# Hidden DFT of three chunks as seven half-size block products, on one Trainium2 core

## The chip, the core and the metric

The kernel runs on one core of a Trainium2 chip. The time is that of the device in microseconds, from a median of repeated executions. Five engines work beside each other, each through its own instructions in order: TensorE (PE, with its weight loads PEld), VectorE (DVE), ScalarE (ACT), GpSimd (POOL) and SyncE (SP), which here only issues DMAs. An instruction that waits for a semaphore holds back everything behind it on its engine.

## What is computed

Four layers, alternating: a Fourier mixing layer A and an MLP layer B, each behind a layer norm, with the residual added. Only A is touched:

```python
def _A_ref(x, dft_seq_re, dft_seq_im, dft_hid_re, dft_hid_im):
    a = jnp.einsum("bsd,ed->bse", x, dft_hid_re)
    b = jnp.einsum("bsd,ed->bse", x, dft_hid_im)
    y = jnp.einsum("ts,bse->bte", dft_seq_re, a) - jnp.einsum("ts,bse->bte", dft_seq_im, b)
    return y
...
x = x + _A_ref(_layernorm(x, axis=-1), A_dft_seq_re, A_dft_seq_im, A_dft_hid_re, A_dft_hid_im)
```

x is 2048 x 512 in float32. The kernel applies the sequence DFT first and the hidden DFT (512 x 512, real and imaginary) after it.

## The kernel before

**Precision.** Every float32 factor is split in two: a "high" part, a cast to fp32r on ACT, and a "low" part, what the cast lost, a subtraction on DVE. A product is three matmuls: high x high, high x low, low x high (`mm3`, L316 to L318).

**Chunks.** The 2048 rows go as four chunks of 512 (c = 0 to 3). The sequence DFT of chunk c takes an x phase (`x_phase`, L498) and a y phase (`y_phase`, L531). The results stand in SBUF as four sums: `im0`, `re1`, `im1`, `re0`. The hidden DFT of chunk c-1 runs inside the x phase of chunk c, as eight calls of `hid` (L593) of 12 matmuls 128x512 each, placed by `HAT` (L40): four calls sum into the two banks PD for the first half of the rows, four for the second.

**The stream.** DFT matrices come as pieces of 512 KB into four raw places (`raw`), DMAs issued by SP. Each becomes one or two *items*, split into a ring of four slots (`ring`). An x phase has 16 items: an even one (kind "plain") feeds 12 matmuls, an odd one (kind "one", a difference of the two halves) 6; in between stand the `hid` calls, each with an item of its own. A y phase has 16 items (`by1`, `by0`) of 12 matmuls. With each item that PE takes (`stream`, L304), the code issues the first stage of the item three further on (`stage_one`: on ACT the cast L260, or on DVE the difference L262 or L266 and then the cast L263 or L267) and the second stage of the item before that one (`stage_two`: DVE low part, L279). A slot is written again when PE is done with the item four back, so both engines wait for PE in the stream. A raw place is loaded again when the stages that read it have been issued.

**Other work beside the stream.** `late` holds lists of functions; `run_late(n)` (L493) issues list n behind item n of the x phase. They hold the last additions to the four sums (L491), their highs (L449) and lows (L452). `add_y` adds the hidden DFT's banks to the residual rows (in `tmp`, called X1) and `y_stats` takes layer norm statistics of them.

What the order of the code is on each engine is the order in which they run: there is no scheduler (`manual_schedule`).

## Time and profile before

| what | value |
|---|---|
| median of 3 runs (lowest to highest) | 1429.8 us (1428.65 to 1429.96) |
| profiled execution: its time, its span | 1430.81 us, 1428.8 us |
| granted TensorE clock over the span | 1.000 |
| DMA moved | 302.13 MB, mean 211 GB/s |
| x phase of chunk 2 in layer 0 | 193.0 to 247.4 us |
| x phases of chunks 1 and 2 in layer 1 | 802.4 to 856.8 us, 900.4 to 954.8 us |

The profiled execution took 1430.81 us, of which 1428.8 us lie between its first and its last instruction; the remaining 2.0 us lie around them. It stands 1.0 us over the median. The busy time of PE says that a matmul was in flight, not that it ran at full rate: matmuls overlap, so their rate is read from one start to the next. Phases are told apart by the tiles of the matmuls: `ax` in an x phase, `ay` in a y phase, `rr` as the stationary operand in the hidden DFT.

### The profile page before, as it was taken

The numbers are of one execution on the slowest core, as the hardware profiler recorded it, in microseconds if no ns is written. First come the engines' busy times: TensorE is split into PE (matmuls) and PEld (weight loads), VectorE is DVE, ScalarE is ACT, GpSimd is POOL, SyncE is SP. The second block draws the span as 40 slices with busy tenths as digits, with TensorE's granted clock in tenths as the row PEclk, the third lists the DMA queues.
The fourth block names the chain that finished last, engine by engine and source line by source line (L and its number), as shares of the span: only waits on it lengthen the run. The fifth ranks groups of instructions, "written<-read, shape, count | busy, mean of one in ns | idle before, by whom it ended". The sixth has DMA issues, their size and how long they took to land.

```text
span 1428.8 us, 17276 instructions
## 1 busy us (share of the span) xinstructions
PE 1422.0 (100%) x6258; PEld 1174.2 (82%) x6258; DVE 1147.5 (80%) x1603; ACT 726.3 (51%) x977; POOL 79.9 (6%) x111
## 2 busy tenths in 40 slices
PE   9999999999999999999999999999999999999998
PEld 7888888888888888888888888888888888888887
DVE  7876997988869888677889979888889698637586
ACT  5553454455465745345554544544555576333352
POOL 2100000001002000000000000000000010000000
PEclk9999999999999999999999999999999999999999
DMA  7426646657664859968755566565676468666594
GB/s 243 140 89 207 206 166 203 204 167 245 225 205 111 287 201 321 379 215 319 240 174 195 168 191 204 186 199 190 205 258 225 137 164 303 209 196 260 168 312 144
DMA packets 136813, 302.13 MB, mean 211 GB/s; under 512 B 15372, under 2 KB 61196, under 8 KB 133528
## 3 DMA queue, kind: packets, MB, share of 16 engines
q1 hardware_dynamic: 132504, 298.93, 63.1%
q10 hardware_dynamic: 4224, 2.10, 0.5%
q8 instruction: 49, 0.80, 0.2%
q14 instruction: 36, 0.29, 0.1%
HBM read 246.18 MB, written 54.81 MB: 211 GB/s over the span
## 4 chain that ended last, share of the span: by engine, by line
PE 95%; DVE 3%; DMA 2%; issue 0%; SPq 0%; ACT 0%; DVEq 0%
PE psd L318 10%; PE psd L316 10%; PE psd L317 10%; PE psa L316 9%; PE psa L318 9%; PE psa L317 9%; PE psc L317 6%; PE psc L318 6%; PE psc L316 6%; PE psb L317 6%; PE psb L318 6%; PE psb L316 6%; DMA raw<-in_ws 1%; DVE ring L279 1%; DMA xs<-in_x 1%; DVE ring1f L266 0%
## 5 line engine op out<-in xcount | busy, mean ns | idle before, releaser
L260 ACT CAST ring<-raw 128x1024 fp32r<-128x1024 f32 x127 | 133.0, 1052 | 98.9 <-PE psd L318 50.1
L279 DVE TENSOR_TENSOR ring<-raw,ring 128x1024 fp32r<-128x1024 f32 (+1 forms) x128 | 154.5, 1211 | 22.5 <-ACT ring L260 22.4
L316 PE MATMUL psd<-ring,rr 128*128 128x512 f32 x208 | 80.9, 389 | 0.0
L317 PE MATMUL psd<-ring,rr 128*128 128x512 f32 x208 | 80.9, 389 | 0.0
L318 PE MATMUL psd<-ring,rr 128*128 128x512 f32 x208 | 80.9, 389 | 0.0
L360 POOL TENSOR_TENSOR rs<-ve,mhalf 128x4 f32<-128x4 f32 x16 | 28.7, 1794 | 578.2 <-DVE nm L359 578.2
L267 ACT CAST ring<-ring0f 128x1024 fp32r<-128x1024 f32 x28 | 29.5, 1054 | 57.1 <-DVE ring0f L266 57.1
L279 DVE TENSOR_TENSOR ring<-ring1f,ring 128x512 fp32r<-128x512 f32 (+1 forms) x56 | 53.2, 949 | 0.8 <-ACT ring L263 0.8
L339 POOL TENSOR_TENSOR rs<-ve,mhalf 128x2 f32<-128x2 f32 (+1 forms) x33 | 30.1, 911 | 396.3 <-DVE nb L338 396.3
L317 PE MATMUL psc<-ring,ay 128*128 128x512 f32 x128 | 50.0, 391 | 0.9 <-DVE ring L279 0.9
L317 PE MATMUL psb<-ring,ay 128*128 128x512 f32 x128 | 50.1, 392 | 0.0
L318 PE MATMUL psc<-ring,ay 128*128 128x512 f32 x128 | 49.8, 389 | 0.0
L318 PE MATMUL psb<-ring,ay 128*128 128x512 f32 x128 | 49.8, 389 | 0.0
L316 PE MATMUL psb<-ring,ay 128*128 128x512 f32 x128 | 49.8, 389 | 0.0
L316 PE MATMUL psc<-ring,ay 128*128 128x512 f32 x128 | 49.8, 389 | 0.0
L267 ACT CAST ring<-ring1f 128x1024 fp32r<-128x1024 f32 x28 | 29.5, 1055 | 39.6 <-DVE ring1f L266 39.6
L317 PE MATMUL psa<-ring,ay 128*128 128x512 f32 x126 | 49.0, 389 | 0.0
L316 PE MATMUL psa<-ring,ay 128*128 128x512 f32 x126 | 49.0, 389 | 0.0
L318 PE MATMUL psa<-ring,ay 128*128 128x512 f32 x126 | 49.0, 389 | 0.0
L316 PE MATMUL psd<-ring,ay 128*128 128x512 f32 x126 | 49.0, 389 | 0.0
L317 PE MATMUL psd<-ring,ay 128*128 128x512 f32 x126 | 49.0, 389 | 0.0
L318 PE MATMUL psd<-ring,ay 128*128 128x512 f32 x126 | 49.0, 389 | 0.0
(575 smaller groups left out, 4375.4 us busy)
## 6 DMA issues: line engine op xcount, KB each, us to landing
raw<-in_ws SPq DMA_DIRECT2D x183, 512.0 KB, 4.9
raw<-in_hs SPq DMA_DIRECT2D x56, 512.0 KB, 3.6
w3b<-w3d SPq DMA_DIRECT2D x15, 1792.0 KB, 9.2
w4r<-w4a SPq DMA_DIRECT2D x33, 512.0 KB, 6.0
wq<-w4a SPq DMA_DIRECT2D x22, 512.0 KB, 4.7
w3d<-w3b SPq DMA_DIRECT2D x5, 1792.0 KB, 6.9
x1d<-tmp SPq DMA_DIRECT2D x12, 512.0 KB, 5.8
xs<-x1d SPq DMA_DIRECT2D x12, 512.0 KB, 6.6
```

The costliest lines, as they stand in the source:

```text
L260: nc.scalar.copy(dest[:, a:b, 0], r[0][:, a:b])
L267: nc.scalar.copy(dest[:, :, 0], lo)
L279: nc.vector.tensor_tensor(lo[:, i], src[:, i], hi[:, i].bitcast(F32), op=ALU.subtract)
L316: nc.tensor.matmul(o, lh, rh, start=first, stop=False, skip_group_check=onto)
L317: nc.tensor.matmul(o, lh, rl, start=False, stop=False, skip_group_check=onto)
L318: nc.tensor.matmul(o, ll, rh, start=False, stop=last, skip_group_check=onto)
L339: nc.gpsimd.tensor_tensor(rs[:, :n], ve[:, :n], mhalf[:, 0, :n], op=ALU.pow)
L360: nc.gpsimd.tensor_tensor(rs, ve, mhalf[:, :, :2], op=ALU.pow)
```

## The change

For three chunks (chunk 1 in layer 0, chunks 0 and 1 in layer 1; `by_seven` names the x phase in which their hidden DFT runs: c = 2 in layer 0, c = 1 and 2 in layer 1) the eight `hid` calls are replaced by seven *units* (`hid_unit`): a block product scheme of the Strassen kind on a 2 x 2 split of both the sums and the DFT matrix. A unit is 24 matmuls with a moving operand of 256 columns instead of 512, so u0 to u6 have 168 matmuls of half width in place of 96 of full width. They stand ahead of item 6 (u0), 8 (u1), 10 (u2), 12 (u3, u4) and 14 (u5, u6).

The parts:

- Seven block matrices (`hd`, in DRAM, 1 MB each with high and low) are made once, in the x phase of chunk 1 in layer 0: three are copied from ring slots by DMAs on ACT's queue (`kept`), four are made by `h_prep` on DVE and ACT. In each of the three phases they are loaded, one for each unit, into two arrays `hwa` and `hwb`, a load waiting for the unit that last read the array.
- `hwa` lies on the raw places 2 and 3. From step 2 of such a phase until u5 is issued (`lent`), the stream has two raw places only (`narrow`).
- The sums stand in `units` (four quarters a11, a21, a12, a22), and differences of quarters are made ahead of the casts (`plan_hid`); each unit's operand gets its own high and low. `im0` is no longer cast in the y phase ahead.
- Two banks take all seven products; `plan_hid` evicts two of them and adds the others to X1, to `pairs` (in `tmp`) and to a second array of residual rows, `x1b`, which is loaded late. Statistics of both move to the y phase that follows.
- One addition in the MLP (`sum_of("t3", ...)`) moves by one point.

```diff
+HUNITS = {3: (0,), 4: (1,), 5: (2,), 6: (3, 4), 7: (5, 6)}
...
+    units, unitsf = both("units", RR, 4, KD, 2, 2 * P)
+    quarter, quarterf = ([v[:, i] for i in range(4)] for v in (units, unitsf))
+    first_diff, first_difff = both("fdiff", EXT, KD, 2, 2 * P)
+    hw = [at("hwa", RAWS + 4 * CH, KD, 2, 2 * P), at("hwb", EXT + 4 * CH, KD, 2, 2 * P)]
...
+    x1b = first_difff[:, 0:2].rearrange("p k r c -> p k (r c)")
...
+    def by_seven(layer, c):
+        return 1 - layer < c < NC - 1
...
-                if c:
+                if c and not by_seven(layer, c):
...
+                if by_seven(layer, c) and k > 1:
+                    narrow.append(p)
...
+            if by_seven(layer, c):
+                narrow.extend(ps[0])
...
+        j = min(range(2 if i in narrow else RAW), key=lambda j: last_in[j])
...
+            if state["lent"] and place[i] > 1:
+                break
...
+        if n in kept:
+            h = kept[n]
+            for u, e in ((2, 0), (5, 1)) if h > 1 else ((0, 0),):
+                v = dest.bitcast(F32)[:, :, :, e * 2 * P : (e + 1) * 2 * P]
+                nc.scalar.dma_start(hd[u][:, h % 2 * 2 : h % 2 * 2 + 2], v)
...
     def x_phase(c, hook):
...
+            if seven:
+                for u in HUNITS.get(k, ()):
+                    hid_unit(u)
+                    for f in loads.pop(u, ()):
+                        f()
+            while c and not seven and h < NP and HAT[h] == k:
...
     def y_phase(c, hook):
...
+                if k == 6 and seven:
+                    load(0)()
...
-                    nc.scalar.copy(im0[0][:, :, 0], im)
+                    if not seven:
+                        nc.scalar.copy(im0[0][:, :, 0], im)
...
+    def h_prep():
...
+        return {
+            2: [load(0), load(1)],
+            3: [load(2), load(3)],
+            5: [total(b22, b12, b22, ALU.add)],
+            6: [total(s2, b22, b11), hi(p, s2)],
+            7: [total(b21, b21, s2)],
+            8: [keep(3, p, s2), total(b12, b11, b12), hi(ka, b12)],
+            9: [keep(4, ka, b12)],
+            10: [hi(p, b22)],
+            11: [keep(1, p, b22)],
+            12: [hi(ka, b21)],
+            13: [keep(6, ka, b21)],
+        }
...
+    HID = (
+        (quarter[0], 1, 0, True),
+        (first_diff, 0, 1, True),
+        (quarter[2], 1, 0, False),
+        (quarter[0], 0, 1, True),
+        (quarter[1], 1, 0, True),
+        (first_diff, 0, 0, False),
+        (quarter[3], 1, 1, True),
+    )
+
+    def hid_unit(u):
+        a, w, b, fresh = HID[u]
+        for part in range(3):
+            for i in range(KD):
+                for t in range(2):
+                    nc.tensor.matmul(
+                        bank_of(PD[b])[:, t],
+                        a[:, i, part == 2, t * P : (t + 1) * P],
+                        hw[w][:, i, part == 1],
...
+    def load(u):
+        return lambda: nc.sync.dma_start(hw[HID[u][1]].bitcast(F32), hd[u])
...
+    def plan_hid(adds, rest_in):
...
+        plan = {
+            1: ["im1-", "re1+"],
+            2: ["re0+", sub(diff, a21, a11), lend(True), load(1)],
+            3: [hi(q11, a11), hi(first_diff, diff)],
+            4: [lo(q11, a11), "im1+"],
+            6: [lo(first_diff, diff), "re0++"],
+            7: [evict(v, 0), sub(a21, a22, a21)],
+            8: [sub(a11, a22, diff), sub(diff, a12, a11)],
+            9: [evict(g, 1), hi(q12, a12), lo(q12, a12), hi(q11, a11), hi(q21, a21)],
+            10: [lo(q11, a11), hi(first_diff, diff), hi(q22, a22)],
+            11: [lo(q21, a21), plus(x1_of[:, 0], x1_of[:, 0], d[0])],
+            12: [lo(first_diff, diff)],
+            13: [
+                plus(v, v, PD[1]),
+                plus(g, g, v),
+                plus(pairs[0][:, 1], g, PD[0]),
+                lo(q22, a22),
+                plus(x1_of[:, 1], x1_of[:, 1], extra_of[0]),
+            ],
+            15: [plus(x1_of[:, 1], x1_of[:, 1], d[0]), plus(pairs[0][:, 0], g, PD[1])],
+        }
...
+        loads.update({0: [load(2)], 1: [load(3)], 2: [load(4)], 3: [load(5)], 4: [load(6)], 5: [rest_in, lend(False), issue_dma]})
...
+                if by_seven(layer, c):
+                    if k == 0:
+                        y_stats(j, X1)
+                    if k == 1:
+                        rows(X1, x1d, j, 2, False)
+                        run_late("x1b")
+                    if k == 2:
+                        y_stats(j + 2, x1b)
+                    if k == 3:
+                        rows(x1b, x1d, j + 2, 2, False)
```

**Where rows move.** Three places in the x phase of chunk 2 in layer 0, each before and after; "waits" names the engines and DMA semaphores that a row waits for. The places are the same in the two phases of layer 1.

SP, the DMA queue, in the last third of the x phase. Before (raw_176 to 179 are raw places 0 to 3; `in_hs` is the hidden DFT's matrix, `in_ws` the sequence DFT's):

```order
L242 DMA raw_176<-in_hs 128x1024 [waits DMAHW6_49,DVE_49]
L242 DMA raw_177<-in_hs 128x1024 [waits DMAHW0_49,DVE_49]
L242 DMA raw_178<-in_ws 128x1024 [waits DMAHW1_49,DVE_49]
L233 DMA x1d<-tmp 128x2x512 [waits DMAHW7_49]
L242 DMA raw_179<-in_ws 128x1024 [waits DMAHW2_49,DVE_49]
L242 DMA raw_176<-in_ws 128x1024 [waits DMAHW3_49,DVE_49]
```

After (raw_191 to 194 are raw places 0 to 3; hd_104, 105 and 106 are the matrices of u4, u5 and u6; fdifff is `x1b`; the pair raw_191, raw_192 here feeds the first two items of the y phase):

```order
L732 DMA hwb<-hd_104 128x2048 [waits DMAHW4_49,PE_49]
L269 DMA raw_191<-in_ws 128x1024 [waits DMAHW5_49,DVE_49,Activation_49]
L732 DMA hwa<-hd_105 128x2048 [waits DMAHW7_49,PE_49]
L732 DMA hwb<-hd_106 128x2048 [waits DMAHW1_49,PE_49]
L269 DMA raw_192<-in_ws 128x1024 [waits DMAHW0_49,DVE_49]
L258 DMA fdifff<-in_x 128x2x512 [waits DMAHW6_49,DVE_49,PE_49]
L269 DMA raw_193<-in_ws 128x1024 [waits DMAHW3_49]
L269 DMA raw_194<-in_ws 128x1024
```

Before, the stream's loads wait for DVE. After, the second half of the first y pair stands behind the load for u6, which waits for PE to end u4, and the pair of the next two y items behind the load of `x1b`, which waits for PE to end u5.

DVE at the end of the same x phase. Before (psd_343 and 344 are the two PD banks; L266 is the first y item's difference):

```order
L491 TENSOR_TENSOR tmp<-psd_343,tmp 128x512
L491 TENSOR_TENSOR tmp<-psd_344,tmp 128x512
L262 TENSOR_TENSOR ring3f<-raw_179 128x512
L279 TENSOR_TENSOR ring_172<-raw_179,ring_172 128x2x512
L266 TENSOR_TENSOR ring0f<-raw_177,raw_176 128x2x512
L279 TENSOR_TENSOR ring_174<-ring3f,ring_174 128x512
```

After (psd_358 and 359 are PD[0] and PD[1]; L293 is the first y item's difference; u5 sums onto PD[0], where u4's product stands until the third `tmp` row has read it):

```order
L747 TENSOR_TENSOR fdiff<-tmp,fdiff 128x4x256
L293 TENSOR_TENSOR ring0f<-raw_192,raw_191 128x2x512
L306 TENSOR_TENSOR ring_189<-ring3f,ring_189 128x512
L537 TENSOR_TENSOR tmp<-tmp,psd_359 128x512
L537 TENSOR_TENSOR tmp<-tmp 128x512
L537 TENSOR_TENSOR tmp<-tmp,psd_358 128x512
L747 TENSOR_TENSOR units<-unitsf,units 128x4x256
L537 TENSOR_TENSOR tmp<-tmp 128x2x256
```

Before, the additions from PD stand ahead of the first y difference. After, they stand behind it, and PE waits for the third of them before u5.

ACT in the middle of the x phase. Before (L449 is a high of one of the sums):

```order
L449 CAST rr_158<-rr11f 128x2x512
L260 CAST ring_174<-raw_176 128x2x512
L260 CAST ring_168<-raw_177 128x2x512
L260 CAST ring_170<-raw_178 128x2x512
L449 CAST rr_152<-rr00f 128x2x512
```

After (L756 evicts a bank, L744 is a high; the first of the three `units` rows is the high of a12, which u2 reads; ring_183 is slot 0, which PE frees with item 8):

```order
L756 COPY tmp<-psd_358 128x512
L290 CAST ring_189<-ring3f 128x512
L287 CAST ring_183<-raw_191 128x2x512
L756 COPY tmp<-psd_359 128x512
L744 CAST units<-unitsf 128x4x256 x3
L290 CAST ring_185<-ring1f 128x512
```

The highs of the operands now stand directly behind the cast of item 12 and an eviction, one item ahead of the unit that reads the first of them.

More of the change, by code (lines that the diff above doesn't have):

```diff
@@ L72, in spectral_mlp_kernel @@
     resd = [dram.tile([D, CH], F32, name=f"resd{i}") for i in range(2)]
+    hd = [dram.tile([P, KD, 2, 2 * P], F32, name=f"hd{i}") for i in range(7)]
     ZW = KD * 2 * SW
@@ L221, in spectral_mlp_kernel @@
             users.setdefault(i, []).append((n, "two" if it[0] == "plain" else "one"))
+    place, before = [], []
+    last_in = [-1 - i for i in range(RAW)][::-1]
+    for i in range(len(pieces)):
+        j = min(range(2 if i in narrow else RAW), key=lambda j: last_in[j])
+        place.append(j)
+        before.append(last_in[j])
+        last_in[j] = i
     raws, slots, sums = {}, {}, {}
-    state = {"dma": 0, "one": 0, "two": 0, "use": 0, "made": 0, "done": 0, "limit": 0, "load": w_pieces[0]}
+    state = {"dma": 0, "one": 0, "two": 0, "use": 0, "made": 0, "done": 0, "limit": 0, "load": w_pieces[0], "lent": False}
     x_left = [(0, 1), (1, 1)] + [(j, 2) for j in range(2, NT, 2)]
@@ L529, in im0_low, with rest_of @@
         nc.vector.tensor_tensor(lo, src, hi.bitcast(F32), op=ALU.subtract)
+    def rest_of(c, xin):
+        return lambda: rows(x1b, xin, c * TC + 2, 2, True)
     def y_phase(c, hook):
-        im = pairs[1] if c == NC - 1 else im0s
+        seven = by_seven(at_layer[-1], c + 1)
+        im0s, re1s, im1s, re0s = sums_of(c)
+        im = wide(pairs[1]) if c == NC - 1 else im0s
         def x1_copies():
@@ L563, in y_phase @@
                         x1_copies()
-                    add(im1s, pairs[0] if c == NC - 1 else re0s, im)
+                    add(im1s, wide(pairs[0]) if c == NC - 1 else re0s, im)
             else:
-                if k == NP - 2 and c < NC - 1:
+                if k == NP - 2 and c < NC - 1 and not seven:
                     im0_low(im)
@@ new lines, in spectral_mlp_kernel @@
+    prep = {}
+    HID = (
[16 more added lines that the diff above has]
+                        hw[w][:, i, part == 1],
+                        start=fresh and part == 0 and i == 0 and t == 0,
+                        stop=part == 2 and i == KD - 1 and t == 1,
+                        skip_group_check=True,
+                    )
@@ new lines, in spectral_mlp_kernel, with lend, hi, lo @@
+    loads = {}
+    def load(u):
+        return lambda: nc.sync.dma_start(hw[HID[u][1]].bitcast(F32), hd[u])
+    def lend(on):
+        return lambda: state.update(lent=on)
+    def plan_hid(adds, rest_in):
+        a11, a21, a12, a22 = (q[:, :, 1] for q in quarterf)
+        diff, sums = (pairs[i].rearrange("p a (b c) -> p (a b) c", b=2) for i in range(2))
+        v, g = (pairs[1][:, i] for i in range(2))
+        x1_of, x1b_of = (wide(t).rearrange("p t h c -> p h t c") for t in (X1, x1b))
+        def hi(o, src):
+            return lambda: nc.scalar.copy(o[:, :, 0], src)
+        def lo(o, src):
+            return lambda: nc.vector.tensor_tensor(o[:, :, 1], src, o[:, :, 0].bitcast(F32), op=ALU.subtract)
+        def sub(o, a, b):
+            return lambda: add(o, a, b, ALU.subtract)
+        def plus(o, a, b):
+            return lambda: add(o, a, b)
+        def evict(o, i):
+            return lambda: nc.scalar.copy(o, PD[i])
+        q11, q21, q12, q22 = quarter
+        d = [bank_of(p) for p in PD]
+        extra_of = bank_of(v), bank_of(g)
+        plan = {
[18 more added lines that the diff above has]
+            15: [plus(x1_of[:, 1], x1_of[:, 1], d[0]), plus(pairs[0][:, 0], g, PD[1])],
+        }
+        for step, todo in plan.items():
+            late[step] = [adds.get(f, lambda: None) if isinstance(f, str) else f for f in todo]
+        loads.update({0: [load(2)], 1: [load(3)], 2: [load(4)], 3: [load(5)], 4: [load(6)], 5: [rest_in, lend(False), issue_dma]})
+        both_halves = pairs[0].rearrange("p h (t c) -> p h t c", t=2)
+        late["x1b"] = [plus(x1b_of, x1b_of, both_halves)]
@@ L1664, in hook @@
                 if layer == 0 and c == 1:
+                    for f in prep.pop(i, ()):
+                        f()
                     if i == 1:
```

102 lines of the change are left out of this document (76 added, 26 removed).

## The prediction

> **What bounds the kernel now.** I read first the page's busy times and chain, then the table of windows by phase, then the timeline inside one x phase.
>
> ```profile
> PE 1422.0 (100%) x6258; PEld 1174.2 (82%) x6258; DVE 1147.5 (80%) x1603; ACT 726.3 (51%) x977; POOL 79.9 (6%) x111
> PE 95%; DVE 3%; DMA 2%; issue 0%; SPq 0%; ACT 0%; DVEq 0%
> ```
>
> PE is the bound: the chain that ended last is 95% PE. So matmuls saved are time saved, if PE then waits for nothing. In the windows (us, then busy us of PE, PEld, DVE, ACT, POOL; granted clock, DMA share, GB/s) the first row is the x phase in which the matrices will be made, then come a changed x phase and the y phase behind it:
>
> ```profile
> 95.00:149.50 54.50, 54.50 (x242) 45.11 (x242) 41.08 (x53) 27.19 (x34) 2.83 (x2) 1.00 0.55 179
> 193.00:247.40 54.40, 54.40 (x242) 45.05 (x241) 44.63 (x54) 26.07 (x31) 2.83 (x2) 1.00 0.56 186
> 247.40:291.00 43.60, 43.60 (x194) 36.12 (x193) 40.33 (x44) 21.41 (x26) 2.23 (x2) 1.00 0.62 201
> ```
>
> PE has no idle time there, but DVE is busy for 82% of the x phase and 92% of the y phase: 9.8 and 3.3 us of slack. Matmul starts, and weight loads in the same stretch:
>
> ```profile
> 150.34 0.39 PE L317 MATMUL psd<-ring,ay 128*128 128x512 f32 x1
> 150.57 0.39 PE L318 MATMUL psd<-ring,ay 128*128 128x512 f32 x1
> 150.80 0.39 PE L316 MATMUL psc<-ring,ay 128*128 128x512 f32 x1
> 150.57 0.19 PEld L316 LDWEIGHTS psc<-ring,ay 128*128 128x128 f32 x1
> ```
>
> One 512-wide matmul starts each 0.227 us (240 of them make the 54.4 us), and a weight load starts with the matmul ahead of it. So an even item is 12 x 0.227 = 2.72 us, an odd one 1.36 us.
>
> **The units.** No row has a 256-wide fp32r matmul. The nearest are the warm-up matmuls: float32 of 128 columns, each with a weight load of its own.
>
> ```profile
> 1.36 5.13 PE L169 MATMUL psd<-ident 128*128 128x128 f32 x24 [1.36 <-POOL mhalf L59]
> 2.37 0.85 PE L169 MATMUL psd<-ident 128*128 128x128 f32 x3
> 2.80 0.64 PE L169 MATMUL psd<-ident 128*128 128x128 f32 x2
> 5.99 0.50 PE L169 MATMUL psd<-ident 128*128 128x128 f32 x3
> 6.10 0.39 PE L169 MATMUL psd<-ident 128*128 128x128 f32 x2
> ```
>
> There are 24, the last three from 5.99 us on. Among the early ones three span 0.85 us and two 0.64, so one starts 0.21 us after another; at the end three span 0.50 and two 0.39, so 0.11. So a weight load can follow another in 0.11 us at the least, and beyond half of the early 0.21 hardly anything is fixed for each matmul, 0.005 us at most. I take the half of 0.227, 0.1133 us, between 0.11 and 0.1133 + 0.005 = 0.118. A unit is then 24 x 0.1133 = 2.72 us, and seven take 19.04 instead of 96 x 0.227 = 21.76: **-2.72 us** for each chunk (-1.9 to -3.3).
>
> [...]
>
> **The waits that the units bring.** Each late function runs behind the stream's rows of its step, and those wait for PE. Rows of the stream and of ACT:
>
> ```profile
> 193.16 0.69 DVE L262 TENSOR_TENSOR ring3f<-raw 128x512 f32<-128x512 f32 x1
> 193.76 1.22 DVE L279 TENSOR_TENSOR ring<-raw,ring 128x1024 fp32r<-128x1024 f32 x1
> 194.90 0.68 DVE L279 TENSOR_TENSOR ring<-ring3f,ring 128x512 fp32r<-128x512 f32 x1
> 195.92 1.05 ACT L260 CAST ring<-raw 128x1024 fp32r<-128x1024 f32 x1 [1.36 <-PE psb L318]
> 203.91 1.99 ACT L260 CAST ring<-raw 128x1024 fp32r<-128x1024 f32 x2
> 190.46 0.62 ACT L263 CAST ring<-ring1f 128x512 fp32r<-128x512 f32 x1 [0.97 <-DVE ring1f L262]
> 190.98 1.05 ACT L260 CAST ring<-raw 128x1024 fp32r<-128x1024 f32 x1
> ```
>
> From start to start, a DVE row of 512 elements takes 0.60 us and one of 1024 1.14; ACT casts take 0.52 and 0.94. The cast at 195.92 belongs to the item that reuses item 0's slot. Item 0 ends 2.72 us behind the phase's start at 193.0, so an engine starts 0.2 us after PE frees a slot.
>
> *u0* stands behind six items, 3 x 4.08 = 12.24 us after the phase's start. It waits for the last addition of step 4, im1+. DVE has ahead of that, from 0.16 us on: 5 short rows and 9 long ones (of the stream's items 2 to 7 five short and three long, then five additions and one low), 5 x 0.60 + 9 x 1.14 = 13.26, so 13.4. With the hand-over PE waits **1.3 us**. If strided operands cost nothing more and two rows find room earlier it is 0; a tenth more on each is 2.
>
> *u1* has its low some 2 us early: nothing. *u2* reads the high of a12, on ACT behind the cast of item 12 (slot of item 8) and an eviction: 0.2 + 0.94 + 0.52 + 1.05 = 2.71 us after item 8, plus 0.15 to hand over; PE has only item 9 to cover it, 1.36. So **1.5 us** (1.3 to 1.8). Its data were there 6 us earlier; it is the row ahead on ACT that counts. *u3* and *u4* have their parts in time, and u4's matrix, loaded after u2, has 6.8 us.
>
> *u5* needs DVE's third addition of step 13, since it sums onto the bank that this row reads. Ahead of it on DVE is the first y difference, which needs raw_192. That DMA stands on SP behind the load for u6, which waits for u4's end. What loads take:
>
> ```profile
> raw<-in_ws SPq DMA_DIRECT2D x183, 512.0 KB, 4.9
> w4s<-w4c SPq DMA_DIRECT2D x5, 1024.0 KB, 4.9
> zt1f<-zd SPq DMA_DIRECT2D x4, 1024.0 KB, 6.2
> L242 SPq DMA_DIRECT2D raw<-in_ws x2: 328/376/424, 245.1 to 245.5; - x2
> DMA to landing us min/median/max: 4.1/4.5/5.0
> DMA to landing us min/median/max: 3.5/4.0/5.0
> ```
>
> The fourth and fifth rows are two loads of 512 KB right behind each other: the second landed 0.87 us further from its issue and was issued 0.38 later, so 512 KB cost 1.25 us of data. The last row is all raw loads of this x phase. So: 0.25 us from u4's end to the issue, 4.9 for 1 MB, 1.25 for raw_192 behind it: 6.4. Then DVE: 1.14 + 0.60 + 3 x 0.60 = 3.54, and 0.15 to hand over: 10.1. PE has items 12 and 13, 4.08. So **6.0 us**. Least: raw_192 lands 3.5 us after an issue 0.38 behind the other, 0.25 + 0.38 + 3.5 + 3.69 - 4.08 = 3.7; most, with 6.2 for the 1 MB: 7.3. *u6* has its operand in time.
>
> **The y phase behind.** Its third and fourth items' pieces and `x1b` are issued after u5's end: 0.25 + 2 x 0.38 + 3.5 + 2 x 1.25 = 7.0 us, or some 6 if the first data start early. DVE then owes four long and two short rows, 5.8 us, before the low of y2. PE has u6, items 14 and 15, y0, y1: 2.72 + 4.08 + 5.44 = 12.2. So DVE enters with no lead, where before it had about 2 us:
>
> ```profile
> 222.09 1.28 DVE L354 BATCH_NORM_STATS2 st<-tmp 128x6 f32<-128x512 f32 x2
> 223.84 1.22 DVE L279 TENSOR_TENSOR ring<-raw,ring 128x1024 fp32r<-128x1024 f32 x1
> 248.47 1.22 DVE L266 TENSOR_TENSOR ring3f<-raw,raw 128x1024 f32<-128x1024 f32 x1
> 249.61 1.22 DVE L279 TENSOR_TENSOR ring<-ring2f,ring 128x1024 fp32r<-128x1024 f32 x1
> ```
>
> A set of statistics is 1.75 us (222.09 to 223.84), a y item 2 x 1.14 = 2.28 on DVE against PE's 2.72. Two sets and the `x1b` addition are 4.64 us within six items, which give back 6 x 0.44 = 2.64. So PE waits **2.0 us** (0, if the lead survives, to 4).
>
> **The rest.** Making the matrices adds 8 long DVE rows, 9.1 us, and 4 ACT casts to the first window, where DVE has 13.4 us of slack; PE's work covers it. I take 1 us once, 0 to 3, as ACT's three sets of copies wait for lows. The dropped cast and low of `im0` free 1.14 us of DVE in a y phase where it then waits for PE. With two raw places a piece has 8 us from free place to use and takes 4.9: nothing. The moved addition and the new views of the same tiles cost nothing beside full PE time.
>
> **Sum.** For each chunk -2.72 + 1.3 + 1.5 + 6.0 + 2.0 = +8.1 us; three chunks +24.2, with the matrices +25.2. The profiled execution would go from 1430.8 to 1456.0 (span 1428.8 to 1454.0). It stands 1.0 over the median of 1429.8, which goes to **1455**. Ends: 3 x (-3.3 + 0 + 1.3 + 3.7 + 0) = +5, so 1435; 3 x (-1.9 + 2 + 1.8 + 7.3 + 4) + 3 = +42.6, so 1472.
>
> **Rivals.**
> - *The short stalls.* SP and the DMAs run ahead of my count: u5 waits 3.7 us, u0 and the y phase nothing or little. +5 to +18: 1435 to 1448. For it: DMAs alone land in 3.5 us. Against it: u6's 1 MB is ahead of raw_192. 0.20.
> - *The clock falls.* PE stands idle for 6 us ahead of u5; today it is idle for 1428.8 - 1422.0 = 6.8 us in all. The rows of the warm-up show PE at half rate from 1.36 to 5.99 us, after a start from rest; so each fall costs 4.6/2 = 2.3 us, three of them 6.9: 1462, with the upper costs 1475. For it: the start's rows. Against it: the granted clock is 1.00 in every window. 0.27. [...]
> - *The waits don't bite: faster.* If DVE and ACT have the late rows done ahead of PE, as they have today's highs and lows, only the units count: 3 x -2.72 = -8.2, 1422. It decides where raw_192 lands: it would have to land before u4 has ended, and stands behind a load that waits for that. 0.05; some 0.03 for an even result, where the waits come to 8 us in all.
> - *Half-width matmuls bound by their weight load* at the row's 0.19 us: 168 x 0.19 - 21.76 = +10 instead of -2.7 for each chunk, 1493. Against it: the 0.11 us pairs. 0.04.
>
> **How the numbers follow.** The forecast, 1448 to 1462, has 0.41. 1455 it is; the range from 1438 to 1474 leaves out the faster and even cases, the load-bound units and a part of the short stalls, under 0.2 in all. A measurement tells 0.2% (2.9 us) from no change: faster 0.05, same 0.03, slower 0.92.
>
> **What would show it.** In the changed trace: starts of `psd<-hwa` and `psd<-hwb` matmuls 0.113 us apart; PE idle ahead of u0 (1.3, released by DVE), u2 (1.5, ACT) and u5 (6, DVE), the y difference before it released by the DMA of raw; 2 us of PE idle in the next y phase; a mean granted clock under 1.00 if it falls. A gap ahead of u5 of under 3 us, or none, makes the prediction wrong.

## The result, and the profile after

| | median (lowest to highest) | runs |
|---|---|---|
| before | 1429.67 us (1428.65 to 1429.96) | 4 |
| after the change | 1490.64 us (1487.12 to 1490.79) | 4 |

The change makes the kernel slower: ratio 1.0422, 95% interval 1.0404 to 1.0440, 61 us. The forecast of 1455 had the sign and its range ended at 1474. The profiled execution of the changed kernel took 1487.12 us, 3.5 under the median; its span is 56.3 us longer than that of before.

From the page of the changed kernel: span, busy time of two engines, and the chain that ended last.

```profile
span 1485.1 us, 17715 instructions
PE 1436.2 (97%) x6474; PEld 1191.8 (80%) x6474; DVE 1161.1 (78%) x1620; ACT 716.9 (48%) x972; POOL 77.8 (5%) x111
PE 86%; DMA 5%; DVE 4%; issue 2%; ACT 2%; SPq 0%; DVEq 0%; ACTq 0%
```

PE has 14 us more busy time although it was given fewer columns, and lies idle 49 us where it had 7; a seventh of the chain is now not PE. Line numbers are those of the changed kernel: L720 is a unit's matmul, L348 to L350 the three matmuls of `mm3`, L537 an addition or subtraction, L744 and L747 the high and low of a quarter, L289, L293 and L306 a stream item's difference and low, L269 its load, L672 a load of the preparation, L311 a kept copy. PE's waits by line, releaser, total, times and longest:

```profile
PE psd L720 <- issue: 23.2, 6, 6.1
PE psd L348 <- DVE tmp L537: 10.9, 3, 4.5
PE psc L349 <- DVE ring L306: 4.1, 3, 3.2
PE psd L720 <- ACT units L744: 3.8, 3, 1.3
```

The first row is the waits ahead of u0 and u5, the fourth that of u2. **The second was not in the prediction**: the y phase's first matmul waits for an addition. "issue" only says that the view found no releaser; the rows around it tell more. PE in chunk 1 of layer 1, start and length in us:

```profile
864.69 3.04 PE L720 MATMUL psd<-hwb,units 128*128 128x256 f32 x24
871.45 0.39 PE L350 MATMUL psa<-ring,ax 128*128 128x512 f32 x1
877.79 4.53 PE L720 MATMUL psd<-hwa,fdiff 128*128 128x256 f32 x24 [5.96 <-issue]
882.16 3.04 PE L720 MATMUL psd<-hwb,units 128*128 128x256 f32 x24
888.92 0.39 PE L350 MATMUL psa<-ring,ax 128*128 128x512 f32 x1
893.76 0.76 PE L348 MATMUL psd<-ring,ay 128*128 128x512 f32 x1 [4.46 <-DVE tmp L537]
894.33 0.63 PE L349 MATMUL psd<-ring,ay 128*128 128x512 f32 x1
894.75 0.63 PE L350 MATMUL psd<-ring,ay 128*128 128x512 f32 x1
```

u4 (864.69) needs 2.88 us to the next matmul's start, 0.120 each; u5 needs 4.37 behind its idle, and the y phase starts with matmuls 0.42 us apart instead of 0.227. The same chunk on SP and on DVE:

```profile
867.76 0.32 SPq L732 DMA_DIRECT2D hwb<-hd  x1
868.17 0.38 SPq L269 DMA_DIRECT2D raw<-in_ws  x1
882.35 0.37 SPq L258 DMA_DIRECT2D fdifff<-x2d  x1
882.78 13.40 SPq L269 DMA_DIRECT2D raw<-in_ws  x6
```

```profile
873.82 1.23 DVE L293 TENSOR_TENSOR ring0f<-raw,raw 128x1024 f32<-128x1024 f32 x1 [8.56 <-DMA raw<-in_ws]
877.00 0.69 DVE L537 TENSOR_TENSOR tmp<-tmp,psd 128x512 f32<-128x512 f32 x1
890.66 1.23 DVE L293 TENSOR_TENSOR ring2f<-raw,raw 128x1024 f32<-128x1024 f32 x1 [8.96 <-DMA raw<-in_ws]
892.94 1.28 DVE L537 TENSOR_TENSOR tmp<-tmp,psd 128x512 f32<-128x512 f32 x2
```

This is one pattern twice. u6's matrix and behind it a piece of the stream (the second half of the first y pair) are issued when u4 ends (867.6); the first y difference can start at 873.82, and the addition that frees u5's bank, queued behind it, ends at 877.69, 0.1 us ahead of u5. When u5 ends (882.2), the next pieces of the stream are issued behind the load of `x1b`; the third y difference waits for them to 890.66, and behind it stand the two additions of the plan's step 15 (its list number 15), the last readers of the banks that the y phase overwrites. PE starts 0.15 us after the first of them ends.

Two windows of the same trace, the one around u5 and the one at the y phase's start, show the clock (the last three columns are granted clock, DMA share, GB/s):

```profile
877.80:885.00 7.20, 7.20 (x48) 7.20 (x49) 3.90 (x4) 1.05 (x1) 0.00 (x0) 0.77 0.17 54
893.80:899.00 5.20, 5.20 (x14) 4.13 (x15) 4.61 (x11) 1.24 (x2) 0.75 (x1) 0.59 0.46 147
```

Where the 56.3 us lie, by the starts of the phases in both traces: 8.2 ahead of the first changed chunk (its x phase starts at 201.2 instead of 193.0), 15.4, 16.2 and 17.3 in the three chunks (x phase 68.1 to 68.8 us instead of 54.4, y phase 45.3 to 46.4 instead of 43.5), and -0.8 in the rest.

The 8.2 us are the preparation of the matrices: 7.1 in the x phase of chunk 1, which takes 61.5 us instead of 54.4, and 1.1 in the y phase behind it. DVE and PE in that x phase, the DMA issues of 95 to 125 us with the median time to landing, and the window of the phase.

```profile
116.08 1.23 DVE L537 TENSOR_TENSOR hrawf<-hrawf 128x1024 f32<-128x1024 f32 x1 [4.11 <-DMA hrawf<-in_hs]
```

```profile
119.10 0.50 PE L349 MATMUL psc<-ring,ax 128*128 128x512 f32 x1 [3.16 <-DVE ring L306]
```

```profile
hd<-ring ACTq DMA_DIRECT2D x6, 512.0 KB, 11.0
hrawf<-in_hs SPq DMA_DIRECT2D x4, 512.0 KB, 10.8
```

```profile
95.00:156.60 61.60, 57.34 (x242) 45.99 (x241) 47.84 (x60) 28.46 (x34) 2.23 (x2) 0.97 0.84 292
```

The window of the same phase before the change:

```profile
95.00:149.00 54.00, 54.00 (x240) 44.69 (x240) 40.58 (x52) 26.69 (x33) 2.83 (x2) 1.00 0.55 179
```

The DMA engines are 84% busy over the phase, not 55%. The trace shows one landing each behind the medians of these two rows: the last of the four loads of 512 KB lands 10.8 us after its issue, where the stream's pieces take 4.8 in the median of the whole run. VectorE stands 4.1 us for the first sum's operand, the stream's lows behind it come late, and PE stands 3.3.

### The profile page after: what moved, and what is told of

Same layout as the page of the kernel before. It is cut to its first block, busy times and chain, and to the rows that moved or that the text cites. A ratio compares the mean times of both kernels' runs of the same rounds, so it can differ in the third digit from the quotient of the medians.

```text
span 1485.1 us, 17715 instructions
## 1 busy us (share of the span) xinstructions
PE 1436.2 (97%) x6474; PEld 1191.8 (80%) x6474; DVE 1161.1 (78%) x1620; ACT 716.9 (48%) x972; POOL 77.8 (5%) x111
## 4 chain that ended last, share of the span: by engine, by line
PE 86%; DMA 5%; DVE 4%; issue 2%; ACT 2%; SPq 0%; DVEq 0%; ACTq 0%
PE psd L348 9%; PE psd L349 8%; PE psd L350 8%; PE psa L349 8%; PE psa L350 8%; PE psa L348 8%; PE psc L349 6%; PE psc L348 6%; PE psc L350 6%; PE psb L349 6%; PE psb L350 5%; PE psb L348 5%; PE psd L720 4%; DMA raw<-in_ws 3%; DVE ring L306 1%
## 5 line engine op out<-in xcount | busy, mean ns | idle before, releaser
L287 ACT CAST ring<-raw 128x1024 fp32r<-128x1024 f32 x103 | 107.8, 1052 | 91.0 <-PE psb L350 36.0
L306 DVE TENSOR_TENSOR ring<-raw,ring 128x1024 fp32r<-128x1024 f32 (+1 forms) x104 | 125.3, 1209 | 12.0 <-ACT ring L287 12.0
L294 ACT CAST ring<-ring0f 128x1024 fp32r<-128x1024 f32 x28 | 29.5, 1054 | 91.1 <-DVE ring0f L293 91.1
L348 PE MATMUL psd<-ring,ay 128*128 128x512 f32 x126 | 50.5, 401 | 10.9 <-DVE tmp L537 10.9
L293 DVE TENSOR_TENSOR ring2f<-raw,raw 128x1024 f32<-128x1024 f32 x28 | 34.2, 1221 | 31.2 <-DMA raw<-in_ws 31.2
L293 DVE TENSOR_TENSOR ring0f<-raw,raw 128x1024 f32<-128x1024 f32 x28 | 34.2, 1221 | 30.4 <-DMA raw<-in_ws 27.7
L294 ACT CAST ring<-ring1f 128x1024 fp32r<-128x1024 f32 x28 | 29.5, 1053 | 56.8 <-DVE ring1f L293 56.8
L306 DVE TENSOR_TENSOR ring<-ring1f,ring 128x512 fp32r<-128x512 f32 (+1 forms) x56 | 53.2, 950 | 0.8 <-ACT ring L290 0.8
L349 PE MATMUL psc<-ring,ay 128*128 128x512 f32 x128 | 51.2, 400 | 0.8 <-DVE ring L306 0.8
L294 ACT CAST ring<-ring2f 128x1024 fp32r<-128x1024 f32 x28 | 29.6, 1056 | 45.1 <-DVE ring2f L293 45.1
L348 PE MATMUL psc<-ring,ay 128*128 128x512 f32 x128 | 51.2, 400 | 0.0
L349 PE MATMUL psd<-ring,ay 128*128 128x512 f32 x126 | 50.3, 399 | 0.8 <-DVE ring L306 0.8
L350 PE MATMUL psc<-ring,ay 128*128 128x512 f32 x128 | 50.8, 397 | 0.0
L306 DVE TENSOR_TENSOR ring<-ring3f,ring 128x1024 fp32r<-128x1024 f32 (+1 forms) x50 | 49.2, 985 | 1.9 <-ACT ring L290 1.7
L350 PE MATMUL psd<-ring,ay 128*128 128x512 f32 x126 | 50.2, 399 | 0.0
L348 PE MATMUL psb<-ring,ay 128*128 128x512 f32 x128 | 50.1, 391 | 0.0
L350 PE MATMUL psb<-ring,ay 128*128 128x512 f32 x128 | 49.8, 389 | 0.0
L348 PE MATMUL psa<-ring,ay 128*128 128x512 f32 x126 | 49.0, 389 | 0.0
L349 PE MATMUL psa<-ring,ay 128*128 128x512 f32 x126 | 49.0, 389 | 0.0
```

What stands on the lines that cost most here:

```text
L287: nc.scalar.copy(dest[:, a:b, 0], r[0][:, a:b])
L293: nc.vector.tensor_tensor(lo, r[1][:, i : i + 1].broadcast_to([P, 2, CH]), r[0], op=ALU.subtract)
L294: nc.scalar.copy(dest[:, :, 0], lo)
L306: nc.vector.tensor_tensor(lo[:, i], src[:, i], hi[:, i].bitcast(F32), op=ALU.subtract)
L348: nc.tensor.matmul(o, lh, rh, start=first, stop=False, skip_group_check=onto)
L349: nc.tensor.matmul(o, lh, rl, start=False, stop=False, skip_group_check=onto)
```

## The experiments

Each median is of 4 runs; the kernel before had medians of 1428.9 to 1430.2 beside them. "Step" is against the kernel that the edit builds on.

| run | median us | ratio to before (95%) | step us |
|---|---|---|---|
| e1, u5's additions earlier | 1461.09 | 1.0213 (1.0196 to 1.0230) | -29.5 on the change |
| e2, the y phase's additions earlier | 1479.90 | 1.0355 (1.0337 to 1.0373) | -10.7 on the change |
| e3, matrix load later | 1478.94 | 1.0345 (1.0329 to 1.0361) | -11.7 on the change |
| e4, before with split matmuls | 1440.54 | 1.0078 (1.0063 to 1.0093) | +11.5 on before |
| e5, e1 and e2 | 1455.63 | 1.0178 (1.0159 to 1.0196) | -5.5 on e1 |
| e6, u0 and u2 too | 1454.75 | 1.0171 (1.0153 to 1.0189) | -0.9 on e5 |
| e7, no preparation | 1444.46 | 1.0106 (1.0090 to 1.0122) | -10.3 on e6 |
| e8, preparation spread | 1461.89 | 1.0228 (1.0211 to 1.0244) | +7.1 on e6 |
| e9, im1+ behind u0 | 1443.20 | 1.0105 (1.0090 to 1.0120) | -11.6 on e6 |
| e10, y phase lightened | 1438.44 | 1.0065 (1.0050 to 1.0080) | -4.8 on e9 |
| e11, kept copies only | 1435.20 | 1.0042 (1.0027 to 1.0057) | -8.0 on e9 |
| e12, sums only | 1442.72 | 1.0089 (1.0072 to 1.0106) | -0.5 on e9 |
| e13, sums one step later | 1445.46 | 1.0111 (1.0096 to 1.0126) | +2.3 on e9 |
| e14, y additions on GpSimd | 1452.89 | 1.0162 (1.0145 to 1.0179) | +7.4 on e13 |

### What u5 and the y phase wait for: e1, e2, e3, e5

e1:

```diff
-            12: [lo(first_diff, diff)],
+            12: [lo(first_diff, diff), plus(v, v, PD[1]), plus(g, g, v), plus(pairs[0][:, 1], g, PD[0])],
             13: [
-                plus(v, v, PD[1]),
-                plus(g, g, v),
-                plus(pairs[0][:, 1], g, PD[0]),
```

> Edit: in the changed kernel's plan the three additions of step 13 that unit u5 waits for (v, g, then the half of the chunk that u5 overwrites) are issued one step earlier, behind lo(first_diff) and ahead of the first y difference. Theory A (the wait before u5 is VectorE's order: the additions stand behind a difference that waits for a chunk of the row of reference data behind u6's matrix load): PE's idle before u5, 6.1 to 6.3 us in each of the three chunks, falls to under 0.5, and the some 20 slow half-wide matmuls behind it (0.21 us apart instead of 0.120, 1.8 us a chunk) go too. The wait before the y phase's first matmul stays at 3 to 5 us. Sum: 3 x (6.2 + 1.8) = 24 us less than the changed kernel, some 1466. Theory B (u5 waits for something that only stands beside the additions, its matrix or the eviction): the idle stays over 4 us and the time stays at 1485 to 1491. Theory C (the waits move on): u5's idle goes but the y phase's start grows by as much; time within 6 us of the changed kernel.

e2:

```diff
-            15: [plus(x1_of[:, 1], x1_of[:, 1], d[0]), plus(pairs[0][:, 0], g, PD[1])],
+            14: [plus(x1_of[:, 1], x1_of[:, 1], d[0]), plus(pairs[0][:, 0], g, PD[1])],
```

> Edit: the two additions of step 15 (the last reads of the two half-chunk sums in PD) are issued in step 14, ahead of the second y difference. Theory A (the wait that the prediction did not have, before the first matmul of the y phase, is for these reads, which stand on VectorE behind a difference that waits for a row chunk): the idle of 2.8 to 4.6 us there falls to about 1 or less, and the 11 or 12 slow full-wide matmuls behind it (some 2.4 us) go. Sum 3 x (3.8 - 0.5 + 2.4) = 17 us less than the changed kernel, some 1473; the idle before u5 stays at 6.1 to 6.3. Theory B (the y phase waits for the split data or the matrix): idle stays, time stays within 3 us of the changed kernel.

e3:

```diff
-            12: [lo(first_diff, diff)],
+            12: [lo(first_diff, diff), load(6)],
...
-        loads.update({0: [load(2)], 1: [load(3)], 2: [load(4)], 3: [load(5)], 4: [load(6)], 5: [rest_in, lend(False), issue_dma]})
+        loads.update({0: [load(2)], 1: [load(3)], 2: [load(4)], 3: [load(5)], 5: [rest_in, lend(False), issue_dma]})
```

> Edit: only the order on SyncE's queue: the load of u6's matrix is issued in step 12 instead of in u4's list, so that the row chunk which the first y difference reads is issued ahead of it and need not stand behind the wait for u4's end. VectorE's order is that of the changed kernel. Theory A (the root of u5's wait is that DMA issue standing behind the matrix load): idle before u5 falls from 6.2 to 0.5 to 3 us, no slow half-wide matmuls behind it, 3 x (4.5 + 1.8) = 14 to 24 us less than the changed kernel, some 1466 to 1477. Theory B (VectorE's own work in front of the additions is too long): idle stays over 5 us, time unchanged. If u6 then waits for its matrix instead, a new idle of up to 5 us before u6 gives most of it back (1480 to 1490).

PE's waits in e1, then in e3:

```profile
PE psd L348 <- DVE tmp L537: 7.7, 3, 2.8
PE psd L720 <- issue: 5.1, 3, 1.8
```

```profile
PE psd L720 <- issue: 15.5, 6, 3.6
PE psd L348 <- DVE tmp L537: 11.3, 3, 4.6
```

In e1 the waits without a releaser ("issue") are three, of 1.8 us at most, all u0's: with the additions ahead of the difference, u5's wait is gone. The slow unit matmuls are gone too (none starts 0.21 us behind the one ahead, 60 do in the changed kernel), and the y phase's start wait shrank by 3.2 us in all, so the gain is 29.5 and not 24. e3 leaves VectorE's order and takes u6's matrix load from ahead of the piece: u5 waits 3.6 to 3.7 instead of 6.2. That is more than the 0.5 to 3 expected, and slow matmuls still follow. In e3 the piece stands behind one more matrix load, that of u5, which waits for u3's end: the two are issued at 862.64 and 862.23, and VectorE waits for the piece until 868.71. Both links of the chain are shown, the matrix loads on SP and the additions behind the difference. In e2 the L348 row is gone from the view, but the gain is 10.7 and not 17, since a new wait comes inside the y phase. Its window of chunk 1 of layer 1:

```profile
885.40:932.60 47.20, 45.13 (x194) 35.77 (x193) 43.65 (x51) 19.79 (x23) 4.46 (x4) 1.00 0.59 194
```

That phase has no start wait and still takes 47.2 us, with VectorE busy 43.65 of them: the idle at its start had, it seems, given VectorE its lead back. e5 is both edits:

> Edit: the changed kernel with both groups of additions ahead of the row differences (those of step 13 in step 12, those of step 15 in step 14). Theory A (the two waits add): the changed kernel less 29.5 (measured for the first alone) less 10.7 (for the second alone) = 1450, and without the idle before the y phase no slow full-wide matmuls there, as much as 3 x 1.5 less again: 1446 to 1452. Idle before u5 under 0.5, before the y phase under 1. Theory B (the time goes to the next wait, VectorE has no lead in the y phase): the differences come later and the ring runs dry in the y phase; over 1455.

It gains 5.5 on e1, less than expected, and its time is that of theory B: the y phases, with no wait at their start, now take 45.9 to 46.0 us instead of 43.5.

### What u0 and u2 wait for: e6, e9

e6, on top of e5:

```diff
-            4: [lo(q11, a11), "im1+"],
+            4: [lo(q11, a11)],
+            5: ["im1+"],
...
-            8: [sub(a11, a22, diff), sub(diff, a12, a11)],
-            9: [evict(g, 1), hi(q12, a12), lo(q12, a12), hi(q11, a11), hi(q21, a21)],
+            8: [hi(q12, a12), sub(a11, a22, diff), sub(diff, a12, a11), lo(q12, a12)],
+            9: [evict(g, 1), hi(q11, a11), hi(q21, a21)],
```

> Edit: the one before, and the addition im1+ in step 5 instead of step 4, the high and low of a12 in step 8 (ahead of and behind the two subtractions) instead of step 9. Theory A (u0 waits only for im1+'s place in VectorE's order, u2 only for the place of a12's high behind a stream cast and an eviction on ScalarE): idle before u0 falls from 1.8 to under 0.5, before u2 from 1.4 to under 0.5; 3 x 2.7 = 8 us less than the run with both additions moved, some 1440. Theory B (u0 waits for something else, its low or its matrix): the idle before u0 stays at 1.8; some 1444.

u2's wait went, u0's grew to 2.2 to 2.5 us, and two of the three brought slow unit matmuls (25 of them 0.21 us apart), which ate the gain. DVE and PE ahead of u0 in e6:

```profile
212.54 1.22 DVE L747 TENSOR_TENSOR units<-unitsf,units 128x1024 fp32r<-128x1024 f32 x1
214.28 1.22 DVE L537 TENSOR_TENSOR unitsf<-unitsf,tmp 128x1024 f32<-128x1024 f32 x1
```

```profile
215.59 3.63 PE L720 MATMUL psd<-hwb,units 128*128 128x256 f32 x20 [2.07 <-issue]
```

The second row is im1+, which ends at 215.50; u0 starts 0.09 us later, 1.8 us behind the low that it does read. e9 puts im1+ behind u0:

```diff
-            5: ["im1+"],
-            6: [lo(first_diff, diff), "re0++"],
+            6: [lo(first_diff, diff), "re0++", "im1+"],
```

> Edit: the kernel without unit waits, with the addition im1+ in step 6, behind u0, instead of step 5, ahead of it. In the run without unit waits u0's idle did not go (2.2 to 2.5 us, against 1.75 to 1.9 before it), and its end moved with im1+'s end. Theory A (u0's first matmul waits for im1+ because the program counts it as the last write to the quarters, though u0 reads another quarter): idle before u0 falls under 0.4, the slow half-wide matmuls behind it (25 in all) go; 3 x (2.2 + 0.7) = 9 us less, some 1446. Theory B (u0 waits for its low or its matrix): unchanged, some 1455.

u0's wait is gone (no gap over 0.2 us there) and 11.6 us with it, more than the 9 expected, since a stretch of slow matmuls in a y phase of e6 (behind 2.2 us of idle at 294 us) did not come again. So u0 had waited for an addition whose result it does not use. That the program takes every write through the name `unitsf` as one to the quarters that u0 reads through `units` is inferred from the order; the runs show that it is im1+'s place that counts.

### What a half-wide matmul costs: e4

```diff
+                hh, ll = rr[ri][dp][:, i, 0, w], rr[ri][dp][:, i, 1, w]
+                for part, (l, r) in enumerate(((hh, 0), (hh, 1), (ll, 0))):
+                    for h in range(2):
+                        cut = slice(h * DH, (h + 1) * DH)
+                        nc.tensor.matmul(
+                            a[:, cut],
+                            l,
+                            s[:, i, r, cut],
...
```

> Edit: the kernel before, with each of the 768 matmuls of 512 columns in the function hid (the product by eight of the three chunks) issued as two of 256 columns; same operands, same result, no other edit. Theory A (the pair's price as the profile of the changed kernel shows it, 0.120 us apart, against 0.227): 768 x (2 x 0.120 - 0.227) = 10 us more than before, some 1440. Theory B (the prediction's step: half the columns, half the time): within 1 us of before. Theory C (a half-wide matmul is held by its weight load, 0.19 us): 768 x (0.38 - 0.227) = 118 us more, some 1547.

The edit costs 11.5 us: 11.5 / 768 = 0.015 us for each matmul that became two. Rows of e4:

```profile
395.78 1.60 PE L601 MATMUL psc<-ring,rr 128*128 128x256 f32 x12
397.22 1.00 PE L601 MATMUL psb<-ring,rr 128*128 128x256 f32 x7
```

12 starts in 1.44 us: 0.120 each. With 0.2267 for 512 columns that is 0.0133 us for each matmul and 0.107 for 256 columns, if the part that does not grow with the columns is the same at both widths. The weight load, 0.19 us in the rows, does not bound it.

### What the preparation costs: e7, e8, e11, e12, e13

e7, on top of e6; e11 and e12 are the parts of it, on top of e9:

```diff
-                prep.update(h_prep())
+                pass
...
-                            if layer == 0 and c == 1 and h < KD:
+                            if layer == 0 and c == 1 and h < 2:
...
-        return lambda: nc.sync.dma_start(hw[HID[u][1]].bitcast(F32), hd[u])
+        return lambda: nc.sync.dma_start(hw[HID[u][1]].bitcast(F32), hd[0])
```

> Edit: the kernel without unit waits, and the preparation of the seven matrices left out (all units read the one matrix that two kept copies make; the four loads, the sums and casts, four of the six kept copies and the four stores of 1 MB are gone), so the output is not the reference's. Theory A (preparation costs what layer 0's first two chunks showed, 7 to 8 us): 7 to 8 us less than the run before, some 1432. Theory B (the prediction's term): 0 to 3 us less, some 1438. If all of the change's cost is waits and preparation, what is left is the products' own gain: before less 3 x (96 x 0.227 - 168 x 0.120) = 4.9, so 1425, plus the y phases' leftover waits.

> Edit: the kernel with im1+ behind u0, and of the matrices' preparation only the six kept copies from the ring stay; the four loads, the sums, casts and stores of 1 MB are left out, and the four units that used them read the first matrix, so the output is not the reference's. The whole preparation costs 10.3 us (the run without it). Theory A (the cost is the ring slots, which the kept copies hold while the DMA engines are full): 2 to 5 us less, since the copies then land in some 5 us instead of 11 but still hold their slots. Theory B (it is the sums and casts, and the loads that VectorE waits for): 8 to 10 us less.

> Edit: the kernel with im1+ behind u0, and of the six kept copies only the first matrix's two stay; the two units of the others read another matrix, so the output is not the reference's. Loads, sums, casts and stores of the preparation stay. Theory A (the ring slots held by the kept copies): 5 to 8 us less than the run with im1+ behind u0. Theory B (the sums and their loads): 0 to 3 us less.

All of it costs 10.3 us, more than both theories of e7 had; the loads, sums, casts and stores are 8.0 (theory B of e11, and of e12), and leaving out four of the six kept copies brings 0.5, within the spread of the runs. The kept copies are not free by themselves: in e11, where they are all that stays, the x phase takes 56.2 us instead of 54.4, and the one whose landing the trace shows takes 10.2 us, with the loads and stores gone. e8 and e13 ask whether it can be placed better (e8 on e6, e13 on e9):

```diff
-            2: [load(0), load(1)],
-            3: [load(2), load(3)],
-            5: [total(b22, b12, b22, ALU.add)],
+            2: [load(0)],
+            3: [load(1)],
+            4: [load(2)],
+            5: [load(3)],
+            7: [total(b22, b12, b22, ALU.add)],
...
-                            if layer == 0 and c == 1 and h < KD:
+                            if layer == 0 and c == 1 and h in (0, 1, 6, 7):
```

> Edit: the kernel without unit waits, and the preparation spread: the four loads of 512 KB one in each of steps 2 to 5 instead of two in 2 and two in 3, sums, casts and stores two steps later (7 to 15), and the four kept copies of the last two blocks taken at those blocks' second passage. Theory A (the preparation costs because its transfers fill the DMA engines between 102 and 122 us, so that ring slots and the loads come 11 us after their issue): the idle of 3.3 us at 115 us and the slow matmuls behind it go; 3 to 6 us less than the run without unit waits, some 1435. Theory B (its instructions on VectorE and ScalarE cost): no change, some 1440.

```diff
-            5: [total(b22, b12, b22, ALU.add)],
-            6: [total(s2, b22, b11), hi(p, s2)],
+            6: [total(b22, b12, b22, ALU.add)],
+            7: [total(s2, b22, b11), hi(p, s2)],
...
```

> Edit: the kernel with im1+ behind u0, and the preparation's sums, casts and stores one step later (6 to 14 instead of 5 to 13); the four loads stay in steps 2 and 3, the kept copies too. Theory A (what the preparation costs is VectorE standing 4.8 us in step 5 for loads that land 11 us after their issue, and the slow matmuls behind PE's idle of 3.9 us): that idle falls under 1, 3 to 5 us less, some 1439. Theory B (its work on VectorE and ScalarE, or transfers of later steps): the wait turns up elsewhere and the time stays within 2 us of 1443.

Both expectations of a gain fell. Of e13's 2.3 us, 1.3 are those by which the kernel before, too, stood higher beside it than beside e9. ACT in e8 and DVE in e13:

```profile
149.43 1.04 ACT L287 CAST ring<-raw 128x1024 fp32r<-128x1024 f32 x1 [6.07 <-DMA hd<-ring]
```

```profile
119.31 1.23 DVE L306 TENSOR_TENSOR ring<-raw,ring 128x1024 fp32r<-128x1024 f32 x1 [5.79 <-DMA raw<-in_hs]
```

In e8 the last two kept copies, issued just behind a store of 1 MB, took 14.0 and 15.9 us to land; a ring slot waits for its copy, and PE stood 9.8 us over two matmuls. In e13 VectorE no longer waits for its sum's operand, but for the stream's own block, which lands late in its turn. The wait moves with the edit; what stays is the traffic: six copies of 512 KB, four loads of 512 KB and four stores of 1 MB, 9 MB more. That the traffic is the cause is not shown: how the 8 us split into loads, stores and VectorE's sums was not separated.

### What the y phases still cost: e10, e14

e10 on e9, then e14 on e13:

```diff
-                        run_late("x1b")
+                        late.pop("x1b", None)
...
-                        y_stats(j + 2, x1b)
+                        for known in (ln1, ln2):
+                            known.update({j + 2: known[j], j + 3: known[j + 1]})
```

> Edit: the kernel with im1+ behind u0, and in the y phases of the three chunks the statistics of the second pair of tiles and the addition for them left out (the first pair's statistics stand in their place), so the output is not the reference's. That is 1.2 + 2.2 = 3.4 us of VectorE's some 43 us in each of these y phases. Theory A (the y phases of 45.9 to 46.6 us, against 43.6 before the change, are held by VectorE, which is busy 42.8 to 43.2 us there and has lost its lead): they fall to 43.6 to 44.5, 3 x 2 = 6 us less than the run with im1+ behind u0. Theory B (the y phases are held by the row transfers): unchanged.

```diff
-        late["x1b"] = [plus(x1b_of, x1b_of, both_halves)]
+        late["x1b"] = [lambda: nc.gpsimd.tensor_tensor(x1b_of, x1b_of, both_halves, op=ALU.add)]
...
-                    add(re0s, re0s, im1s)
+                    if by_seven(at_layer[-1], c):
+                        nc.gpsimd.tensor_tensor(re0s, re0s, im1s, op=ALU.add)
+                    else:
+                        add(re0s, re0s, im1s)
```

> Edit: the run before, and in the y phases of the three chunks two additions of 128x1024 (re0 + im1, and that of the second pair of tiles) on GpSimd instead of VectorE; the result is the reference's. Theory A (VectorE holds these y phases, as leaving out 3.4 us of its work showed, 4.8 us in all): 2.4 us less on VectorE a phase, 3 to 4 us less in all than the run before, some 1436. Theory B (GpSimd takes so long, or slows VectorE so much, that its result is waited for): no gain or a loss. For a time below the kernel before, 1429, preparation and y phases would have to cost nothing: the products alone are worth 4.9.

Chunk 1 of layer 1 (x phase and y phase) in e9, and its y phase in e10:

```profile
811.10:864.40 53.30, 53.12 (x314) 47.19 (x312) 43.70 (x48) 23.61 (x32) 0.00 (x0) 1.00 0.68 247
864.40:910.40 46.00, 44.60 (x194) 35.91 (x193) 43.28 (x51) 19.80 (x23) 4.46 (x4) 1.00 0.61 195
```

```profile
863.50:908.00 44.50, 44.37 (x194) 36.09 (x194) 40.85 (x44) 19.85 (x23) 2.23 (x2) 1.00 0.61 203
```

With its waits gone, the x phase is 1.1 us shorter than before the change (54.4): the products do gain. The y phase is 2.3 us longer, and loses most of that when VectorE's busy time falls from 43.28 to 40.85. So VectorE's load is most of it. The late pieces have a part too: VectorE waits 2.2 us for one of them in that phase of e9, 0.9 in the kernel before, and how much of the rest is theirs was not separated. e14 gave two additions to GpSimd and lost; its rows on GpSimd and on DVE:

```profile
876.57 3.32 POOL L786 TENSOR_TENSOR fdifff<-fdifff,tmp 128x1024 f32<-128x1024 f32 x1
```

```profile
876.41 1.22 DVE L293 TENSOR_TENSOR ring1f<-raw,raw 128x1024 f32<-128x1024 f32 x1
877.54 3.43 DVE L306 TENSOR_TENSOR ring<-ring0f,ring 128x1024 fp32r<-128x1024 f32 x1
```

The three y phases of e14 are 1.4 to 3.2 us longer than those of e13. No run came below the kernel before. e9 with both of e10's and e11's gains would be 1443.2 - 4.8 - 8.0 = 1430.4, an estimate, and it would still have to do the work that those leave out.

## Why the prediction had the sign and missed the size

The terms, for one chunk as the mean of three, from the traces. A wait is taken here from start to start of the matmuls around it, less their usual spacing, and so stands some 0.15 us above the idle time in the views:

| term | predicted us | measured us |
|---|---|---|
| seven units against eight products | -2.72 | -1.60 (21.76 - 168 x 0.120) |
| u0's wait | 1.3 | 1.84 (1.75 to 1.90) |
| u2's wait | 1.5 | 1.41 |
| u5's wait | 6.0 | 6.21 (6.12 to 6.26) |
| y phase | 2.0, inside it | 3.81 (2.83 to 4.62), ahead of it |
| slow clock | none (a rival) | 3.8 (3.1 to 4.4) |
| sum | 8.1 | 15.5, of 16.3 that the chunk grew |
| matrices, once | 1 | 8.2 |

Point by point:

- **Waits of u0, u2 and u5: right**, in place, cause and size. e1, e3 and e9 show the causes: the additions behind the difference, the piece of the stream behind the matrix load, im1+ ahead of u0 (u0 does not use im1+'s result, which the prediction did not ask). u2's went with its high's move in e6. No row of before gives the hand-overs of 0.15 us to PE and 0.25 us to the DMA issue that the sums use: in the changed trace the three units start 0.05 to 0.10 us after the row that they wait for, and the load behind u4 is issued 0.19 us after the start of the matmul that follows u4.
- **"PE has u6, items 14 and 15, y0, y1": this step failed.** It let the y phase start freely, and asked only when VectorE would have y2's low. But y0 overwrites the banks that step 15's additions read last, and those stand behind the third y difference, for which the prediction had itself counted the late pieces. e2 shows it: with these additions ahead of the second difference the wait is gone. The same question that found u5's wait, who reads this bank last and behind what, was not asked of y0: 3.8 us a chunk in the place of 2.0. The 2.0 inside the phase were right in mechanism: once the start wait is gone (e5, e9) the phases take 45.0 to 46.1 us instead of 43.5, and e10 shows that VectorE's load is most of it.
- **"PE's work covers it. I take 1 us once": mis-sized**, 8.2 measured, 8.0 to 10.3 by leaving it out. It counted instructions on VectorE and ScalarE against their slack, and none of the 9 MB of transfers in a phase whose DMA engines were 55% busy before. What of that makes the 8 us stays open.
- **The clock rival (0.27) came true, and cost more than its price.** It was priced at one fall of 2.3 us a chunk; there were two in each, behind u5's wait and behind the y phase's, 11.4 us in the three chunks and 1.6 more in the preparation. Under e9, with no such idle in the chunks, the granted clock is 1.00 in both windows shown, and no stretch of slow matmuls lies in the three chunks. The fall itself stands in the trace of the changed kernel: 0.59 granted in the window behind 4.6 us of idle. It also came behind less idle than the 6 us that the rival started from: slow matmuls followed 2.83 us of idle ahead of a y phase there, and 2.00 us in e5, while u0's waits of 1.75 to 1.90 us had none behind them.
- **Half the columns were not half the time**: 0.120 us for 0.1133, 1.1 us a chunk. The weight-load rival (0.19 us) is out by e4.
- "Short stalls" and "the waits don't bite" are out: u5 waited at the forecast's length in all three chunks.

Of the 35.6 us between forecast and median, the trace gives the y phase's start 3 x 1.8, the clock 3 x 3.8, the units 3 x 1.1, u0, u2 and u5 together 3 x 0.7, the matrices 7.2, the rest of the chunks 3 x 0.8, and -0.8 outside them, 31 in all; 3.5 more is the profiled run's place below its median, and 1.0 that of the profiled run of before above its own. The range was too narrow since its upper end took each listed wait at its worst, but no cost that was not on the list, and the clock only as a rival.

## What to carry to other kernels

For every bank or place that a moved step overwrites, name its last reader on each engine and the row that this reader is queued behind; do it for the phase after the change, too, since the wait sits where the bank is next used. Cost added transfers by the share of the DMA engines that they fill in their own phase (here 84% instead of 55%), not only by the instructions around them. Where a change leaves PE idle for 2 us or more, count slow matmuls behind it as a possible price (here they followed some idles of 2.0 to 3.5 us and all longer ones, at 1.0 to 2.5 us each time), and check a change's gain first at the price of its own matmul shape: here it was 4.8 us in all, and the waits of u0, of u5 and of the y phase were each worth more.

## What the runs showed of the hardware

- **The clock fell behind short idles.** In the changed kernel the granted clock is 0.50 from 877.79 to 880.60 us, behind 6.12 us of idle, and from 893.76 to 897.60, behind 4.62 (idle taken as in the table above), and 1.00 from 839.20 to 842.00, behind 1.75. In the traces of all runs together, the start of the program aside, no idle under 2.0 us was followed by slow matmuls, all over 3.5 us were, and in between some were and some not (2.00 us in e5 was; 2.45 in e7 and 3.47 in e2 were not). The slow stretch was then 12 to 27 half-wide or 5 to 12 full-wide matmuls, 2 to 6 us long.
- **A fixed part of a matmul shows at the full clock, and not in the slow stretches.** 256 and 512 columns start 0.120 and 0.227 us apart at full clock (changed kernel and e4), 0.213 and 0.427 in the slow stretches of the changed kernel: in proportion to the columns there, with 0.0133 us on top at full clock. These are matmuls with fp32r operands and a weight load each.
- **An addition on GpSimd and the VectorE row beside it held each other up.** The addition of 128x1024 took 3.3 us on GpSimd against 1.22 on VectorE, and the VectorE row beside it 3.43 instead of 1.22 (e14). In all six such places GpSimd ends 2.25 to 2.27 us after the VectorE row that it started beside, and the held VectorE row ends 1.1 us after GpSimd, as if each had waited for the other's end. That each waited is a reading of these times; no run shows what held them.
